# Negated maxima of the first six heads on ScalarE's DMA queue instead of SyncE's

## The chip, the cores and the metric

The kernel runs on one core of one Trainium2 chip. The core has five engines with an instruction queue each: TensorE (PE in the profile, with its weight loads as PEld), VectorE (DVE), ScalarE (ACT), GpSimd (POOL) and SyncE (SP), which computes nothing and only issues DMAs. Transfers that SP or ACT issue run on the same 16 DMA engines, on a queue for each issuer (q1 and q10 of the profile). The metric is the device time of one execution in microseconds (us); smaller is better.

## The reference

Block-sparse attention over 4 x 8 heads of 768 positions and 64 features, then a feed-forward layer on the 3072 tokens:

```python
scores = scale * np.matmul(q, k.transpose(0, 1, 3, 2))
...
scores = np.where(mask, scores, -1000000000.0)
scores = scores - np.max(scores, axis=-1, keepdims=True)
attn = np.exp(scores)
attn = attn / (np.sum(attn, axis=-1, keepdims=True) + 1e-09)
return np.matmul(attn, v).astype(np.float32)
...
h = x @ w_in
g = h - np.tanh(h)
return (g @ w_out).astype(np.float32)
```

The maximum of each query's scores is subtracted ahead of the exponential. The change concerns the way on which those maxima reach TensorE.

## The kernel before

There are 32 heads, two to a pair `pr`. A pair's transposed queries and keys lie in one of three buffers, `slot0` to `slot2` (`pr % 3`), each with four parts `sA`, `sB`, `sC`, `sD`: the masked high words, and products of high and low words for more precision. `sA` has a row of ones (row 88), and row 88 of `sB` holds the negated maximum of each query. A score is the sum of two matmuls: one over `sC` and `sD` (128 rows), one over rows 0 to 88 of `sA` and `sB` (89 rows). The second adds the negated maximum within the contraction, so it cannot start before that row has been written.

The maxima of a head come from a first pass over its scores, ahead of the second one:

- `smax` (PE): matmuls over rows 0 to 87 (88 rows in the profile) into one of six PSUM banks.
- `most` (DVE): a maximum over each bank, tile `mc`; `most_join` (DVE) joins six columns, tile `mj`.
- `most_turn` (PE): transposes `mj`, so that 6 x 128 values lie along rows.
- `most_send` (DVE, then SP): negates and shifts them into tile `nm`, and issues a DMA of 6 x 128 floats (3 KB) from `nm` into row 88 of `sB`.

The second pass of a head is three steps `n` of three tiles each: `scores` (PE), `exps` (ACT, tile `pe`, 512 columns each), `high` (ACT, tile `ph`, a 16-bit copy, two to a step), `low` (POOL, tile `pl`), `accum` (PE, over `ph`, `pl` and the values `vhl`), and at a head's end `norm` (DVE). The first passes run ahead of the second by `LEAD`, less so at the start (`RAMP`).

Nearly all other transfers stand on SP's queue: loads of queries and keys (`rawx`) and values (`rawv`), copies of `rawx` and of its low words `lo` into the slots (`dist`), and the attention results on their way to memory (`xscr<-xq`, from `spill`). Before the change ACT issues four loads at the start and one store at the end.

The order is set by hand. `at(time, f, args)` files a call under a due time, in steps of which two make one `n`; the list is sorted by time, and a helper (the line L91 that nearly all rows of the profile have) keeps each engine's instructions in the order in which they are written. An engine works its queue in order: an instruction that waits holds all behind it. A DMA has one more wait, because each takes the next of eight completion semaphores (DMAHW0 to DMAHW7) in the order of the program, over both queues, and must find that the last user of that semaphore has landed.

The pattern repeats for all heads to the end of the attention (the last nm is issued at 346.2 us); after that come the feed-forward units, which the change leaves as they are.

Of the kernel before, what the change touches and what calls it, by code (L numbers as in the profile page):

```python
# [64 lines left out]
TAIL, LASTN = 90, 93  # L65
SPIN = (-40, 14), (-1.95, 6), (-0.2, 2), (3.1, 3), (3.5, 1)
RAMP, NRAMP = 4, 24
LATE = {2: (10, 10, 6), 3: (8, 9, 3), 4: (5, 8, 2), 5: (2, 4, 1), 6: (1, 2, 0.5)}

THR2 = 0.16  # L70
# [34 lines left out]
@with_exitstack  # L105
def attention_ffn(ctx, tc, kq, v, samp, w_in, w_out, blocks, out):
    nc = tc.nc
    cst = ctx.enter_context(tc.tile_pool(name="cst", bufs=1))
    dpool = ctx.enter_context(tc.tile_pool(name="dpool", bufs=1, space=DRAM))
    xscr = [dpool.tile([P, T, DM], F32, name=f"xscr{b}") for b in range(B)]  # L110

    ident = cst.tile([P, P], F32, name="ident")
    make_identity(nc, ident)
    bias = [cst.tile([P, 1], F32, name=f"bias{i}") for i in range(2)]
    for x, val in zip(bias, (QB, THR2)):
        nc.vector.memset(x, val)

    slots = [cst.tile([P, 4, 2, S], F32R, name=f"slot{i}") for i in range(NSLOT)]
    wt = {(m, ft): dpool.tile([P, 512], F32, name=f"w{m}{ft}") for ft in range(NPRE) for m in "io"}
    part = [dpool.tile([P, DM], F32, name=f"part{j}") for j in range(CT)]  # L120
    f2 = ctx.enter_context(tc.tile_pool(name="f2", bufs=2))
    px = ctx.enter_context(tc.tile_pool(name="px", bufs=2))
    ffn = FFN(tc, w_in, w_out, xscr, ident, bias, slots, wt, out, f2, part, px)
    psum = ctx.enter_context(tc.tile_pool(name="psum", bufs=1, space=PSUM))
    banks = [psum.tile([P, 512], F32, name=f"ps{i}") for i in range(8)]
    ffn.banks, ffn.hb, ffn.cv, ffn.xt = banks[:4], banks[4:6], banks[6], banks[7]
    with ExitStack() as actx:
        turn = iter(range(10**6))
        ps = lambda n=6: banks[next(turn) % n], banks[6:]
        ffn.nc = InOrder(tc)  # L130
        attention(actx, tc, kq, v, samp, w_in, w_out, blocks, xscr, ident, ps, slots, wt, px, f2, ffn)
        ffn.nc = InOrder(tc, InOrder.ENGINES[:4])
    with ExitStack() as fctx:
        ffn.rest(fctx)


def attention(ctx, tc, kq, v, samp, w_in, w_out, blocks, xscr, ident, ps, slots, wt, px, f2, ffn):
    nc = InOrder(tc)
# [164 lines left out]
    mcs, sms = {}, {}  # L303
# [30 lines left out]
    def most_send(h):  # L334
        pr, j = divmod(h, 2)
        nm = p2.tile([T, P], F32R, tag="nm", name=f"nm{h}")
        nc.vector.tensor_scalar(out=nm, in0=mcs.pop(h), scalar1=-1.0, scalar2=8.0 * PBITS * math.log(2.0), op0=ALU.mult, op1=ALU.add)
        nc.sync.dma_start(
            out=sB[pr % NSLOT].bitcast(F32)[88:89, j, :].rearrange("o (t c) -> o t c", t=T), in_=nm.bitcast(F32)
        )  # L340

# [72 lines left out]
    def at(time, f, *args):  # L414
        ev.append((time, len(ev), f, args))
# [19 lines left out]
    for pr in range(NPAIR):  # L435
        t0 = 12 * pr
        late = LATE.get(pr, (0, 0, 0))
        at(t0 - 34.2 + late[0] if pr > 1 else -26.6 if pr else -49, load_x, pr)
# [27 lines left out]
    def smt(n):  # L466
        return 2 * n - LEAD + RAMP * max(0, 1 - n / NRAMP)

    for h in range(2 * NPAIR):
        t0 = smt(3 * h + 2)  # L470
        late = 0 if h < 4 else 0.8
        at(t0 + (2.65 if h > 4 else 1.6), most_join, h)
        at(t0 + 2.5 + late, most_turn, h)
        at(t0 + 2.75 + late, most_send, h)
        for step in range(3):
            at(6 * h + 10.3 + 0.5 * step, norm, h, step)
    for n in range(6 * NPAIR):
# [378 lines left out]
```

## Time and profile before

| what | value |
|---|---|
| three timed runs | 892.28, 892.74, 894.45 us, median 892.74 |
| the profiled execution, its own time | 895.38 us |
| its span, first to last instruction | 893.6 us |
| mean granted clock of TensorE | 0.998 |
| transfers on SP's queue (q1) | 95.31 MB, 86764 packets |
| transfers on ACT's queue (q10) | 1.05 MB, 464 packets |
| share of the chain that ended last | PE 80%, DVE 10%, DMA 5% |

In a row of a timeline stand the start, the length, the engine (SPq and ACTq are DMA issues), the operation, the tiles out and in, and the count of merged instructions; in brackets the engine's idle time before it and what ended it. Tile names leave out buffer numbers. Times count from the start of the span.

### The profile page before, as it was taken

The numbers are of one execution on the slowest core, as the hardware profiler recorded it, in microseconds if no ns is written. First come the engines' busy times: TensorE is split into PE (matmuls) and PEld (weight loads), VectorE is DVE, ScalarE is ACT, GpSimd is POOL, SyncE is SP. The second block draws the span as 40 slices with busy tenths as digits, with TensorE's granted clock in tenths as the row PEclk, the third lists the DMA queues.
The fourth block names the chain that finished last, engine by engine and source line by source line (L and its number), as shares of the span: only waits on it lengthen the run. The fifth ranks groups of instructions, "written<-read, shape, count | busy, mean of one in ns | idle before, by whom it ended". The sixth has DMA issues, their size and how long they took to land.

```text
span 893.6 us, 18523 instructions
## 1 busy us (share of the span) xinstructions
PE 875.4 (98%) x7078; PEld 734.8 (82%) x7078; DVE 717.8 (80%) x1262; ACT 648.6 (73%) x1080; POOL 505.8 (57%) x266
## 2 busy tenths in 40 slices
PE   7899999999999999999999999999999999999997
PEld 6778878888888888878888888888888888888885
DVE  8888899999999988998997687676668666866664
ACT  5799989999999999777776655565556555555553
POOL 7788989999999995677775222222222222222222
PEclk9999999999999999999999999999999999999999
DMA  6787788887888865347420202120102010001001
GB/s 182 191 212 182 182 218 206 204 210 193 211 214 222 199 173 175 117 142 225 140 76 34 63 7 66 30 34 15 47 5 34 10 47 1 1 1 48 0 1 47
DMA packets 87316, 97.53 MB, mean 109 GB/s; under 512 B 41764, under 2 KB 62436, under 8 KB 87228
## 3 DMA queue, kind: packets, MB, share of 16 engines
q1 hardware_dynamic: 86764, 95.31, 40.9%
q10 hardware_dynamic: 464, 1.05, 0.5%
q8 instruction: 55, 0.90, 0.4%
q14 instruction: 33, 0.27, 0.1%
HBM read 44.64 MB, written 15.20 MB: 67 GB/s over the span
## 4 chain that ended last, share of the span: by engine, by line
PE 80%; DVE 10%; DMA 5%; issue 2%; ACT 2%; POOL 1%; SPq 1%; ACTq 0%; DVEq 0%; POOLq 0%
PE ps L91 80%; DVE mc L91 4%; DVE ps L91 2%; DMA rawx<-kq 1%; DMA slot<-nm 1%; DVE lo L91 1%; DMA stage<-w_out 1%; DMA slot<-rawx 1%; ACT pe L91 1%; DMA rawv<-v 1%; SPq L91 1%; ACT ph L91 1%; DVE xq L91 1%; DVE pl L91 1%; DVE cvti L91 0%
## 5 line engine op out<-in xcount | busy, mean ns | idle before, releaser
L91 POOL TENSOR_TENSOR pl<-pe,ph 128x1536 f16<-128x1536 f32 x90 | 287.2, 3206 | 33.6 <-ACT ph L91 22.0
L91 POOL TENSOR_TENSOR gl<-t,gh 128x512 fp32r<-128x512 f32 x96 | 125.0, 1302 | 309.0 <-ACT gh L91 293.0
L91 PE MATMUL ps<-slot 128*128 128x512 f32 (+5 forms) x1224 | 257.7, 355 | 9.0 <-DMA slot<-nm 2.2
L91 PEld LDWEIGHTS ps<-slot 128*128 128x128 f32 (+2 forms) x1224 | 186.8, 191 | 38.0 <-DVE mc L91 4.1
L91 DVE TENSOR_REDUCE mc<-ps 128x1 f32<-128x512 f32 (+1 forms) x288 | 192.4, 680 | 21.4 <-PE ps L91 20.0
L91 ACT ACTIVATE u<-ps 128x512 f32<-128x512 f32 x96 | 57.4, 598 | 197.7 <-PE ps L91 197.7
L91 ACT ACTIVATE pe<-ps 128x512 f32<-128x512 f32 x288 | 164.0, 586 | 17.6 <-PE ps L91 14.4
L91 PE MATMUL ps<-slot,wx 128*128 128x512 f32 x720 | 173.0, 389 | 0.0
L91 ACT ACTIVATE ph<-pe 128x768 f16<-128x768 f32 x187 | 157.6, 843 | 5.4
L91 PEld LDWEIGHTS ps<-slot,wx 128*128 128x128 f32 x720 | 135.2, 188 | 28.0
L91 PE MATMUL ps<-wx,gh 128*128 128x512 f32 x480 | 147.9, 389 | 0.0
L91 PEld LDWEIGHTS <-ph 128*128 128x128 f16 x2304 | 112.6, 97 | 16.1 <-issue 13.1
L91 DVE TENSOR_TENSOR t<-t,ps 128x512 f32<-128x512 f32 x74 | 50.7, 685 | 88.1 <-ACT t L91 88.1
L91 PE MATMUL ps<-vhl,ph 128*128 128x65 f16 (+1 forms) x2304 | 120.6, 195 | 0.0
L91 PE MATMUL ps<-vhl,pl 128*128 128x65 f16 x1152 | 116.3, 193 | 0.6 <-DVE pl L91 0.3
L91 PEld LDWEIGHTS <-pl 128*128 128x128 f16 x1152 | 107.2, 100 | 1.0 <-POOL pl L91 0.6
L91 PEld LDWEIGHTS ps<-wx,gh 128*128 128x128 f32 x480 | 90.1, 188 | 18.5
L91 PE MATMUL ps<-wx,gl 128*128 128x512 f32 x240 | 93.5, 389 | 0.0
L91 DVE COPY_PREDICATED t<-mk,ps 128x512 f32<-128x512 int32 x96 | 71.3, 743 | 6.7 <-ACT mk L91 0.4
L91 DVE TENSOR_TENSOR ps<-ps,u 128x512 f32<-128x512 f32 x96 | 66.6, 694 | 11.5 <-ACT hs L91 11.4
L91 DVE SCALAR_TENSOR_TENSOR ps<-qq,ps 128x512 f32<-128x512 f32 x96 | 66.6, 694 | 8.0 <-DVE ps L91 0.5
L91 PE MATMUL ps<-slot,slot 128*128 128x512 f32 x288 | 69.6, 391 | 0.6 <-DVE t L91 0.6
(103 smaller groups left out, 1186.6 us busy)
## 6 DMA issues: line engine op xcount, KB each, us to landing
slot<-rawx SPq DMA_DIRECT2D x31, 384.0 KB, 7.1
slot<-lo SPq DMA_DIRECT2D x62, 192.0 KB, 3.1
slot<-rawx SPq DMA_DIRECT2D x61, 192.0 KB, 4.1
rawx<-kq SPq DMA_DIRECT2D x15, 768.0 KB, 6.1
stage<-w_in SPq DMA_DIRECT2D x13, 512.0 KB, 3.8
stage<-w_out SPq DMA_DIRECT2D x13, 512.0 KB, 4.0
rawv<-v SPq DMA_DIRECT2D x16, 384.0 KB, 5.3
xscr<-xq SPq DMA_DIRECT2D x16, 384.0 KB, 3.6
```

What stands on the lines that cost most here:

```text
L91: r = f(*args, **kw)
```

## The change

The transfer leaves `most_send` and becomes a call of its own, `most_dma`. For heads 0 to 5 it is issued by ACT and filed 0.3 later than the negation; for the other 26 heads it stays on SP at the same due time.

```diff
+EARLYH = 6
...
-        nc.sync.dma_start(
+        mcs[h] = nm
+
+    def most_dma(h):
+        pr, j = divmod(h, 2)
+        nm = mcs.pop(h)
+        (nc.scalar if h < EARLYH else nc.sync).dma_start(
             out=sB[pr % NSLOT].bitcast(F32)[88:89, j, :].rearrange("o (t c) -> o t c", t=T), in_=nm.bitcast(F32)
         )
...
         at(t0 + 2.75 + late, most_send, h)
+        at(t0 + 2.75 + late + (0.3 if h < EARLYH else 0), most_dma, h)
```

The order of the instructions on TensorE, VectorE and GpSimd stays the same; those of ACT and SP differ at the six transfers. Three places show it. Each row is an instruction with its tiles, and in brackets the semaphores that it waits for: an engine's name for that engine's, DMAHW with a number for a transfer's. The line number of the helper is L91 before and L92 now.

SP's queue at the first head, before: the loads of pair 1's keys and queries and pair 0's values, the two copies of pair 0's low words, the transfer of `nm0`, and the first copies for pair 1.

```order
L91 DMA rawx1_173<-kq 128x1536 [waits DMAHW1_49]
L91 DMA rawv0_175<-v 128x768 [waits DMAHW2_49]
L91 DMA slot0_73<-lo0_160 64x768 [waits DMAHW3_49,Pool_49]
L91 DMA slot0_73<-lo0_160 64x768 [waits DMAHW4_49]
L91 DMA slot0_73<-nm0_232 1x6x128 [waits DVE_49]
L91 DMA slot1_74<-rawx1_173 64x2x768 [waits DMAHW1_49]
L91 DMA slot1_74<-rawx1_173 64x2x768 [waits DMAHW7_49]
```

The same place of SP's queue now.

```order
L92 DMA rawx1_173<-kq 128x1536 [waits DMAHW1_49]
L92 DMA rawv0_175<-v 128x768 [waits DMAHW2_49]
L92 DMA slot0_73<-lo0_160 64x768 [waits DMAHW3_49,Pool_49]
L92 DMA slot0_73<-lo0_160 64x768 [waits DMAHW4_49]
L92 DMA slot1_74<-rawx1_173 64x2x768 [waits DMAHW1_49]
L92 DMA slot1_74<-rawx1_173 64x2x768
```

The transfer of `nm0` is gone from SP, and the copies for pair 1 follow the low words directly. The numbers also show how the semaphores are dealt: 1, 2, 3, 4 to four transfers in turn, so the first copy of the low words has number 3.

ACT's queue at the same head, between the placing of pair 0's low words and the first exponentials, now (before, the row of `nm0` isn't there, and the others stand in the same order):

```order
L92 ACTIVATE slot0_73<-slot0_73 64x768 [waits DMAHW7_49]
L92 ACTIVATE slot0_73<-lo0_160 64x768 [waits Pool_49] x2
L92 DMA slot0_73<-nm0_232 1x6x128 [waits DMAHW3_49,DVE_49]
L92 ACTIVATE pe0_255<-ps2_97 128x512 [waits PE_49]
L92 ACTIVATE pe0_255<-ps4_99 128x512 [waits PE_49]
```

On ACT the transfer waits for VectorE, as before, and also for number 3, which belongs to the first copy of the low words.

ACT's queue at head 1, before: the end of step 1 and the start of step 2, whose exponentials are `pe2`.

```order
L91 ACTIVATE ph1_309<-pe1_294 128x768 [waits Activation_49]
L91 ACTIVATE pe1_294<-ps3_98 128x512 [waits PE_49]
L91 ACTIVATE ph1_309<-pe1_294 128x768 [waits Activation_49]
L91 ACTIVATE pe2_336<-ps2_97 128x512 [waits PE_49]
L91 ACTIVATE pe2_336<-ps4_99 128x512 [waits DVE_49,PE_49]
```

The same place now.

```order
L92 ACTIVATE ph1_309<-pe1_294 128x768 [waits Activation_49]
L92 ACTIVATE pe1_294<-ps3_98 128x512 [waits PE_49]
L92 ACTIVATE ph1_309<-pe1_294 128x768 [waits Activation_49]
L92 DMA slot0_73<-nm1_328 1x6x128 [waits DMAHW0_49,DVE_49]
L92 ACTIVATE pe2_336<-ps2_97 128x512 [waits PE_49]
L92 ACTIVATE pe2_336<-ps4_99 128x512 [waits PE_49]
```

The transfer of `nm1` stands between the last copy of step 1 and the exponentials of step 2, and both wait for it to be issued. The transfers of heads 2, 3 and 5 also stand directly behind a `ph` copy on ACT, that of head 4 behind the third `pe` of step 10.

## The prediction

> **What bounds the kernel now.** I read the busy times of the page first, then busy time by stretch, then the chain of waits, then single engines' timelines.
>
> ```profile
> PE 875.4 (98%) x7078; PEld 734.8 (82%) x7078; DVE 717.8 (80%) x1262; ACT 648.6 (73%) x1080; POOL 505.8 (57%) x266
> 14.00:27.00 13.00, 9.93 (x55) 7.51 (x53) 12.50 (x26) 8.74 (x14) 10.43 (x10) 1.00 0.81 219
> 27.00:33.00 6.00, 3.69 (x49) 2.92 (x50) 5.49 (x10) 2.96 (x5) 5.61 (x2) 1.00 1.05 247
> 90.00:110.00 20.00, 19.69 (x275) 16.88 (x274) 17.55 (x36) 19.25 (x30) 19.09 (x7) 1.00 0.70 170
> 130.00:180.00 50.00, 49.54 (x690) 42.59 (x687) 47.51 (x100) 47.98 (x75) 46.27 (x15) 1.00 0.83 211
> 400.00:600.00 200.00, 199.78 (x882) 164.87 (x881) 156.20 (x244) 129.86 (x235) 91.14 (x72) 1.00 0.29 77
> ```
>
> The stretches give PE, PEld, DVE, ACT and POOL busy, then the granted clock, the DMA engines' share and GB/s. TensorE works 875.4 of 893.6 us, and from 130 us on it hardly pauses (49.54 of 50, 199.78 of 200). So an early delay or gain is a shift that is carried to the end; the early stages decide. From 14 to 27 us VectorE is the bound (12.50 of 13) and TensorE idles 3.07 us; from 27 to 33 us TensorE idles 2.31 us.
>
> Next, who waits for the moved transfers (tile nm), and two pieces of the chain of waits (start, length):
>
> ```profile
> L91 SPq DMA_DIRECT2D slot<-nm x32: 730/747/797, 15.5 to 346.2; - x32
>   PE ps L91: 2.2, 2
> 27.08 5.04 DMA slot<-nm
> 61.53 6.00 DMA slot<-nm
> 32.16 1.60 PE L91 MATMUL ps<-slot 89*128 89x512 f32 x7 [1.61 <-DMA slot<-nm]
> 67.57 1.10 PE L91 MATMUL ps<-slot 89*128 89x512 f32 x5 [0.57 <-DMA slot<-nm]
> ```
>
> TensorE waits twice for nm, 2.2 us in all: 1.61 us for head 1 (issued 27.08, landed 5.04 us later) and 0.57 us for head 4 (61.53, 6.00 us). That is the pool from which the change can draw directly. Heads 2, 3 and 5 make nobody wait.
>
> The first stall costs twice. These stretches of 3.41 us lie on the clock's own steps:
>
> ```profile
> 19.65:23.06 3.41, 2.64 (x14) 1.86 (x13) 3.17 (x8) 3.35 (x6) 1.39 (x1) 1.00 0.90 232
> 26.48:29.89 3.41, 2.50 (x44) 1.99 (x43) 3.38 (x7) 3.18 (x5) 3.11 (x1) 1.00 1.04 267
> 29.89:33.30 3.41, 1.80 (x11) 1.29 (x10) 2.94 (x5) 0.59 (x3) 3.10 (x1) 1.00 1.04 235
> 33.30:36.71 3.41, 3.41 (x42) 2.89 (x41) 1.38 (x3) 2.71 (x5) 0.56 (x1) 0.50 0.78 171
> ```
>
> The stretch with the stall has TensorE busy for 1.80 of 3.41 us, and the next one runs at clock 0.50 throughout, with TensorE as the bound: 3.41 x 0.5 = 1.7 us lost. A stretch with 2.50 busy was not followed by that.
>
> **Part 1, heads 1 and 4: faster landing.** On SP, nm stands behind bulk loads in one queue. On ACT's queue nothing stands before it. What such a transfer takes there is not in the trace; the bounds are a lone one and a queued one:
>
> ```profile
> 16.00:18.00 2.00, 1.16 (x6) 0.71 (x5) 1.86 (x4) 0.03 (x1) 2.00 (x4) 1.00 0.27 60
> 15.46 0.80 SPq L91 DMA_DIRECT2D slot<-nm  x1
> 16.88 1.05 PE L91 MATMUL ps<-slot 128*128 128x512 f32 x2 [0.76 <-DMA slot<-lo]
> 17.43 0.19 PEld L91 LDWEIGHTS ps<-slot 89*128 89x128 f32 x1 [0.40 <-DMA slot<-nm]
> 27.70 0.95 PE L91 MATMUL ps<-slot 128*128 128x512 f32 x3 [0.91 <-DVE mc L91]
> ```
>
> Head 0's took 17.43 - 15.46 = 1.97 us while the DMA engines were mostly idle (0.27 from 16 to 18 us); the other end is 6.00. I take 2.5, nearer the lone one, since the queue is empty though the DMA engines are not. Head 1 needs it within 32.16 - 1.61 - 27.08 = 3.47 us, so its 1.61 us go; head 4 within 6.00 - 0.57 = 5.4, so its 0.57 go. The half-clock stretch goes with the first: another 1.7 us of this execution.
>
> By the Trainium skill, DMA: Bandwidth & Descriptors, section Issuing engines are not separate DMA queues, starting DMAs from several engines saves only the sequencer's time, usually small beside the DMA. By that rule the 5.04 and 6.00 us would stay, and with them both stalls. The section on queues, rings and completion order of the same page says that SP and ACT own a ring each on every DMA engine and that the engines go round between rings, which would let nm pass the bulk loads. No run here shows either yet.
>
> **Part 2, head 0: later issue.** Each transfer takes the next of eight completion semaphores and waits until that one's last user has landed. With nm now later in the program's order, head 0's gets the semaphore of the first lo transfer (DMAHW3 in the rows ahead), where before it waited for VectorE alone. TensorE's wait for lo ends at 16.88, so ACT issues at about 16.8 rather than 15.46: 1.34 us later. With the 2.5 us from above instead of 1.97, head 0's scores start at about 19.3 instead of 17.43: **1.9 us late** (bounds: 1.34, and 16.8 + 6.00 - 17.43 = 5.4). Queued behind that matmul on TensorE are the maxima matmuls of head 1, and VectorE waits for those:
>
> ```profile
> 17.03 2.59 DVE L91 TENSOR_REDUCE mc<-ps 128x1 f32<-128x512 f32 x4
> 26.78 0.27 DVE L91 TENSOR_SCALAR nm<-ps 6x128 fp32r<-6x128 f32 x1
> 13.01 1.11 SPq L91 DMA_DIRECT2D slot<-lo  x2
> 16.30 4.87 SPq L91 DMA_DIRECT2D slot<-rawx  x4
> ```
>
> VectorE is full there (12.50 of 13), so nearly all of the 1.9 us reaches head 1's nm at 26.78 and TensorE's matmul at 27.70, which waits for VectorE. It is a loss in full against the 1.61 won. SP, freed of nm, can send the rawx copies right behind the lo issues, which end at 14.12, instead of at 16.30; nobody waits for them, but they load the DMA engines while nm travels, which is why I don't take 1.97.
>
> The longer gap can also cost clock. TensorE would idle 0.76 + 1.9 = 2.7 us around 16 to 19.3, more than the 1.61 before 33 us. A half-clock stretch then holds 1.71 of the 2.64 us of work that stands in 19.65 to 23.06: 0.9 us late (bounds 0, if none follows, and 1.7). I take 0.9.
>
> By the Trainium skill, TensorE: Matmul & The Clock Gate, Part 1, the clock falls to half after an idle window of about 3.4 us. The trace differs: 1.80 of 3.41 us busy was enough. By the page's rule this term would be nil and the forecast 892.7.
>
> **Part 3, ACT's time.** Six issues at 0.75 us move to ACT's sequencer:
>
> ```profile
> SPq L91 <- DVE mc L91: 23.5, 6, 8.6
> 0.75 2.48 ACTq L91 DMA_DIRECT2D rawx<-kq  x4
> 25.59 0.85 ACT L91 ACTIVATE ph<-pe 128x768 f16<-128x768 f32 x1
> 26.34 1.09 ACT L91 ACTIVATE pe<-ps 128x512 f32<-128x512 f32 x2
> 32.75 1.08 ACT L91 ACTIVATE pe<-ps 128x512 f32<-128x512 f32 x2 [2.81 <-PE ps L91]
> 50.34 0.84 ACT L91 ACTIVATE ph<-pe 128x768 f16<-128x768 f32 x1
> 51.09 0.58 ACT L91 ACTIVATE pe<-ps 128x512 f32<-128x512 f32 x1
> ```
>
> An issue on ACT took 2.48 / 4 = 0.62 us in the one place that the trace shows. Head 0's falls into ACT's idle time before its first exponential. Head 1's blocks ACT from 26.44 until nm is made (26.78 + 0.27 = 27.05) and 0.75 more: the exponentials at 26.34 start near 27.8, 1.5 us late, and 2.81 us of idle time behind them take that up. Heads 2 to 5 come where ACT is full. Each activation starts before the last one ends (26.34 against 25.59 + 0.85 = 26.44), so ACT's sequencer is an instruction ahead, and heads 2, 3 and 5 stand right behind a ph copy of 0.84 us that covers 0.75. I take 0.2 us for the four, bounds 0 and 4 x 0.75 = 3.0. SP loses waits of up to 8.6 us for maxima (23.5 in all), and its loads go earlier; as no engine waits for those loads in these stretches, I count nothing for it. If that cover were gone, a load would show as a wait in the stretches up to 80 us.
>
> **Sum.** Against the profiled execution (895.38 us: span 893.6 and 1.8 around it): -1.61 - 0.57 - 1.7 + 1.9 + 0.9 + 0.2 = -0.9, so 894.5. That execution lies 2.64 us above the median of the runs shown (892.74). The three runs are 892.28, 892.74 and 894.45; I read the gap of about 2 us as the half-clock stretch, present in the third and in the profiled run and absent at the median. Then 1.7 of the 2.64 is not there to be won, and the other 0.9 is profiling's own offset: 894.5 - 0.9 = **893.6 us**. In the same terms, the median gains 2.18 and loses 3.0.
>
> **The rivals.**
> - *Cheap head 0.* nm lands near 1.97 us, and no half clock follows its gap: -2.18 + 1.34 + 0.2 = -0.6, so 892.1; if VectorE's slack hides even the 1.34, 890.6. For it: ACT's queue is empty. Against: VectorE's 12.50 of 13, and 0.81 DMA share in that stretch. Stages bound by ACT up to 110 us (19.25 of 20) may swallow some of it.
> - *Loaded landing* (ends slower). On ACT's queue nm still takes 5.04 us, because the DMA engines are loaded and not because of the place in a queue. Head 0 is then 16.8 + 5.04 - 17.43 = 4.4 us late, head 1's stall stays but for 0.04, and head 4's goes: 4.4 - 0.04 - 0.57 + 0.9 + 0.2 = +4.9, so 897.6. Each 1 us of landing costs 1 us, and twice that from 3.47 us on; the sum passes +2.7 at a landing of 3.9 us. For it: SP's loads now start before nm. Against: 1.97, and the queue of its own.
> - *Bare ACT time.* The sequencer isn't ahead, and four issues cost 3.0 where ACT is full: 893.6 + 2.8 = 896.4. For it: 19.25 of 20. Against: the overlapped starts.
> - *The change does nothing for the landing.* Each head's landing stays what it was on SP (1.97, 5.04, 6.00): head 0 pays 1.34, both stalls remain, and 0.2 is added: 894.3.
>
> **How the numbers follow.** Chances: forecast 0.56 (own range 891.5 to 895.3), cheap head 0 0.20, loaded landing 0.11, bare ACT time 0.08, no effect on the landing 0.05. A measurement of this kernel can tell about 0.3% (2.7 us) from no change. Faster than 890.06 is only the far end of cheap head 0: 0.06. Slower than 895.42 are most of loaded landing (0.09) and of bare ACT time (0.06) and a tail of the forecast (0.01): 0.16. The rest, 0.78, is within. The range runs from 890.5 (all of cheap head 0 but its tail) to 896.5 (bare ACT time), and leaves out loaded landing.
>
> **What would show it.** Right: head 0's first 89-row matmul moves from 17.43 to 18.7 or later, waiting for nm; the waits of 1.61 and 0.57 are gone; nm's issues stand on ACT's queue with no new idle time of ACT behind them from 40 to 75 us; a clock of 0.50, if any, stands near 19 to 24 us and not at 33. Wrong: landings on ACT's queue of 4 us and more, a wait for nm still at 32 us, PE waiting for ACT's pe or ph by more than 1 us between 42 and 76 us, or head 0 no later than before.

## The result, and the profile after

The changed kernel takes 902.18 us (median of 4 runs, 900.24 to 902.77), the kernel before 892.51 (4 runs, 892.10 to 894.45): ratio 1.0101, 95% interval 1.0082 to 1.0119. It is slower by 1%, where 893.6 and no measurable change were forecast. The profiled execution takes 901.92 us, with a span of 900.1.

The waits for nm come first. The views are the answer on the tile nm (issues with their count and minimum, median and maximum in ns; waits in us with their count), the chain of waits (start, length) and TensorE's timeline.

```profile
L92 ACTq DMA_DIRECT2D slot<-nm x6: 677/692/1282, 16.9 to 79.2; - x6
  PE ps L92: 6.2, 2
```

```profile
16.93 4.87 DMA slot<-nm
42.91 6.07 DMA slot<-nm
```

```profile
21.84 2.50 PE L92 MATMUL ps<-slot 89*128 89x512 f32 x8 [4.38 <-DMA slot<-nm]
49.03 3.47 PE L92 MATMUL ps<-slot 89*128 89x512 f32 x11 [1.82 <-DMA slot<-nm]
```

There are two waits again, but others: head 0 (4.38 us) and head 2 (1.82 us) in place of head 1 (1.61) and head 4 (0.57), 6.2 us instead of 2.2. The transfers of heads 0 and 2 needed 4.87 and 6.07 us on a queue on which nothing stood before them.

The first three stretches are those of the prediction's table, the fourth is the one in which it read a DMA share of 0.27; below them stand three of the clock's own steps. All are of the kernel after:

```profile
14.00:27.00 13.00, 7.22 (x31) 5.60 (x30) 7.25 (x16) 3.35 (x5) 5.25 (x7) 0.74 0.94 259
27.00:33.00 6.00, 4.30 (x26) 3.24 (x24) 5.89 (x12) 4.94 (x8) 5.56 (x3) 1.00 0.16 35
130.00:180.00 50.00, 48.74 (x681) 41.82 (x681) 46.70 (x100) 47.30 (x74) 43.84 (x15) 1.00 0.80 202
16.00:18.00 2.00, 0.59 (x3) 0.19 (x1) 1.92 (x4) 0.00 (x0) 2.00 (x4) 1.00 0.96 221
18.69:22.10 3.41, 0.26 (x1) 0.26 (x2) 0.00 (x0) 0.00 (x0) 0.56 (x1) 0.50 1.05 237
22.10:25.52 3.42, 3.42 (x13) 3.03 (x14) 1.83 (x3) 2.04 (x3) 0.00 (x0) 0.50 1.00 347
49.41:52.83 3.42, 3.42 (x21) 2.71 (x20) 1.68 (x3) 2.54 (x5) 3.42 (x2) 0.50 0.91 187
```

From 14 to 27 us VectorE works 7.25 us instead of 12.50, and TensorE 7.22 instead of 9.93. Three steps run at clock 0.50. The DMA engines are at 0.94 there instead of 0.81, at 0.96 instead of 0.27 from 16 to 18, and at 0.16 from 27 to 33, where before they stood at 1.05: the loads have moved forward, into the time in which head 0's nm travels.

SP's queue shows why, around head 2. Before:

```profile
30.35 0.73 SPq L91 DMA_DIRECT2D slot<-rawx  x1
39.16 0.74 SPq L91 DMA_DIRECT2D slot<-nm  x1
39.95 0.43 SPq L91 DMA_DIRECT2D rawx<-kq  x1
40.42 2.71 SPq L91 DMA_DIRECT2D slot<-rawx  x4
```

```profile
39.00:41.00 2.00, 2.00 (x43) 1.85 (x42) 1.56 (x6) 1.88 (x3) 0.27 (x1) 1.00 0.02 5
```

After:

```profile
35.63 0.54 SPq L92 DMA_DIRECT2D rawx<-kq  x1
36.21 6.30 SPq L92 DMA_DIRECT2D slot<-rawx  x5
42.85 0.84 ACT L92 ACTIVATE ph<-pe 128x768 f16<-128x768 f32 x1
42.91 0.68 ACTq L92 DMA_DIRECT2D slot<-nm  x1
```

```profile
42.90:49.00 6.10, 4.30 (x64) 3.53 (x60) 4.67 (x12) 5.54 (x8) 3.23 (x2) 1.00 0.99 217
```

Before, SP reached nm after the issue of a copy at 30.35 and stood there until VectorE had made nm at 39.13. For those 8 us nothing behind it was issued, the DMA engines emptied (0.02 from 39 to 41), and nm went ahead of the loads. After, SP does not wait for nm: pair 3's load and the copies are issued from 35.63 on, ahead of nm at 42.91, and the DMA engines are at 0.99 while it travels. So the wait on SP's queue, which looked like lost time, had kept the way free for nm.

### The profile page after: what moved, and what is told of

Read it like the earlier page. It is cut to its first block, busy times and chain, and to the rows that moved or that the text cites. A ratio compares the mean times of both kernels' runs of the same rounds, so it can differ in the third digit from the quotient of the medians.

```text
span 900.1 us, 18528 instructions
## 1 busy us (share of the span) xinstructions
PE 876.3 (97%) x7078; PEld 735.1 (82%) x7078; DVE 717.7 (80%) x1262; ACT 649.0 (72%) x1080; POOL 505.3 (56%) x266
## 4 chain that ended last, share of the span: by engine, by line
PE 81%; DVE 9%; DMA 4%; issue 2%; ACT 2%; POOL 1%; SPq 0%; ACTq 0%; DVEq 0%; POOLq 0%
PE ps L92 81%; DVE mc L92 3%; DVE ps L92 2%; DMA slot<-nm 1%; DVE pl L92 1%; DMA rawo<-w_out 1%; ACT pe L92 1%; DMA rawv<-v 1%; ACT ph L92 1%; DVE lo L92 1%; DVE xq L92 0%; DMA rawx<-kq 0%; DMA wo<-cvto 0%; DVE ph L92 0%; DVE cvti L92 0%
## 5 line engine op out<-in xcount | busy, mean ns | idle before, releaser
L92 POOL TENSOR_TENSOR pl<-pe,ph 128x1536 f16<-128x1536 f32 x90 | 287.0, 3203 | 40.3 <-ACT ph L92 24.8
L92 POOL TENSOR_TENSOR gl<-t,gh 128x512 fp32r<-128x512 f32 x96 | 124.6, 1298 | 309.2 <-ACT gh L92 293.2
L92 PE MATMUL ps<-slot 128*128 128x512 f32 (+5 forms) x1224 | 259.6, 357 | 14.2 <-DMA slot<-nm 6.2
L92 PEld LDWEIGHTS ps<-slot 128*128 128x128 f32 (+2 forms) x1224 | 188.4, 192 | 43.2 <-DMA slot<-nm 7.0
L92 DVE TENSOR_REDUCE mc<-ps 128x1 f32<-128x512 f32 (+1 forms) x288 | 192.1, 678 | 27.6 <-PE ps L92 26.2
L92 ACT ACTIVATE u<-ps 128x512 f32<-128x512 f32 x96 | 57.6, 600 | 197.6 <-PE ps L92 197.6
L92 ACT ACTIVATE pe<-ps 128x512 f32<-128x512 f32 x288 | 164.1, 587 | 23.7 <-PE ps L92 19.0
L92 PE MATMUL ps<-slot,wx 128*128 128x512 f32 x720 | 172.9, 389 | 0.0
L92 ACT ACTIVATE ph<-pe 128x768 f16<-128x768 f32 x187 | 157.6, 843 | 5.6
L92 PEld LDWEIGHTS ps<-slot,wx 128*128 128x128 f32 x720 | 135.2, 188 | 28.0
L92 PE MATMUL ps<-wx,gh 128*128 128x512 f32 x480 | 147.8, 389 | 0.0
L92 PEld LDWEIGHTS <-ph 128*128 128x128 f16 x2304 | 111.9, 97 | 16.2 <-issue 13.2
L92 DVE TENSOR_TENSOR t<-t,ps 128x512 f32<-128x512 f32 x74 | 50.6, 684 | 88.3 <-ACT t L92 88.3
L92 PE MATMUL ps<-vhl,ph 128*128 128x65 f16 (+1 forms) x2304 | 119.9, 194 | 0.0
L92 PE MATMUL ps<-vhl,pl 128*128 128x65 f16 x1152 | 115.6, 192 | 1.1 <-POOL pl L92 0.8
L92 PEld LDWEIGHTS <-pl 128*128 128x128 f16 x1152 | 106.8, 99 | 1.4 <-POOL pl L92 1.0
L92 PEld LDWEIGHTS ps<-wx,gh 128*128 128x128 f32 x480 | 90.1, 188 | 18.6
L92 PE MATMUL ps<-wx,gl 128*128 128x512 f32 x240 | 93.4, 389 | 0.0
L92 DVE COPY_PREDICATED t<-mk,ps 128x512 f32<-128x512 int32 x96 | 71.1, 741 | 6.7 <-ACT mk L92 0.4
L92 DVE TENSOR_TENSOR ps<-ps,u 128x512 f32<-128x512 f32 x96 | 66.6, 693 | 11.5 <-ACT hs L92 11.4
L92 DVE SCALAR_TENSOR_TENSOR ps<-qq,ps 128x512 f32<-128x512 f32 x96 | 66.6, 694 | 8.1 <-DVE ps L92 0.5
L92 PE MATMUL ps<-slot,slot 128*128 128x512 f32 x288 | 69.5, 390 | 0.6 <-DVE t L92 0.6
```

Of the source, the lines that this page charges most:

```text
L92: r = f(*args, **kw)
```

## The experiments

The theory after the two traces is that the place of nm among the loads counts, not the queue or the engine that issues it. Its rivals: ScalarE's queue is slow by itself; ScalarE's own time for the issues; the wait for a completion semaphore; the half clock. Times are medians, and the difference in us is against the runs of the kernel before on the same chip.

| run | us | minus before | 95% interval of the ratio |
|---|---|---|---|
| head0_back | 899.00 | +6.27 | 1.0059 to 1.0083 |
| head0_alone | 897.78 | +5.05 | 1.0046 to 1.0072 |
| held_loads | 897.96 | +5.23 | 1.0042 to 1.0078 |
| heads_1_4 | 897.76 | +5.03 | 1.0043 to 1.0069 |
| head1_alone | 893.03 | +0.41 | 1.0001 to 1.0018 |
| head2_alone | 896.43 | +3.81 | 1.0026 to 1.0051 |
| held_until_landed | 896.19 | +3.57 | 1.0024 to 1.0050 |
| nm0_behind_loads | 898.82 | +6.20 | 1.0058 to 1.0085 |
| heads_0_2_held | 896.27 | +3.68 | 1.0028 to 1.0053 |
| head0_filled | 900.59 | +8.00 | 1.0077 to 1.0104 |
| loads_behind_nm1 | 897.74 | +5.15 | 1.0043 to 1.0068 |
| copies_behind_nm1 | 891.90 | -0.47 | 0.9984 to 1.0010 |
| head0_filled_less | 896.54 | +4.17 | 1.0039 to 1.0081 |

### Which heads cost: head0_alone, head2_alone, head1_alone, head0_back

The edit is to the changed kernel, here for head 0 alone; `2,`, `1,` and `1, 2, 3, 4, 5` are the other three.

```diff
-EARLYH = 6
+EARLYH = 0,
...
-        (nc.scalar if h < EARLYH else nc.sync).dma_start(
+        (nc.scalar if h in EARLYH else nc.sync).dma_start(
...
-        at(t0 + 2.75 + late + (0.3 if h < EARLYH else 0), most_dma, h)
+        at(t0 + 2.75 + late + (0.3 if h in EARLYH else 0), most_dma, h)
```

> Only head 0's transfer on ScalarE's queue, heads 1 to 5 on SyncE's as before. Theory L: landing again over 4 us, TensorE waits about 4.4 us for it, half clock at 19 to 25 us; the small stalls of heads 1 and 4 may stay. 896 to 899, i.e. 4 to 6 us over the kernel before. Rival S (the wait for the semaphore of the first copy of the low words, 1.4 us, is what head 0 pays, and the long landing of the one profile was chance): 893.5 to 894.5, landing about 2 us. Rival A: no loss, within 0.5 us of before.

> Only head 2's transfer on ScalarE's queue; before it made nobody wait (made 39.13, issued 39.16, last packet 1.46 us later). Theory P: ScalarE comes to it 0.7 to 0.9 us late, behind a ph copy, and with SyncE's loads no longer held behind it the last packet comes 4 to 7 us after the issue; TensorE waits 1.5 to 4 us for it and a half-clock step of 3.4 us follows; 895.5 to 899. If the loss in the changed kernel was handed on from head 0 and head 2 is late only because of it: within 1 us of the kernel before.

> Only head 1's transfer on ScalarE's queue, where with heads 1 and 4 moved it was issued as soon as it was made (27.14, issued 27.17) and removed the wait at 32 us. Theory P (a transfer on ScalarE's queue loses its place: it is issued when ScalarE's queue comes to it, and its packets share the DMA engines with loads that on SyncE's queue would stand behind it; a head wins only where neither happens): head 1 alone wins its 1.61 us or a part, and the later heads, which are on SyncE's queue again, keep landing in under 2 us but for head 4; 890.5 to 892.7. Rival (any transfer on ScalarE's queue costs, by ScalarE's time or by a mixture of queues): 894 or more.

> Head 0's transfer back on SyncE's queue, heads 1 to 5 stay on ScalarE's. Theory L (a maximum that leaves on ScalarE's queue meets the bulk loads that SyncE, no longer held by it, sends at the same moment; heads 0 and 2 pay): head 0's 4.38 us wait of TensorE and the half-clock steps at 19 to 25 us go; head 1 lands in under 3.5 us, so the 1.61 us of before stay away; head 2's wait near 49 us (1.82 us) and its half-clock step stay. 902.2 less about 5.5: 895 to 898. Rival Q (ScalarE's queue is slow by itself, 3 to 6 us whatever the load): the same here, so this run doesn't part them. Rival A (ScalarE's own time for the issues): heads 1 to 5 still cost it, 900 or more.

Head 0 alone costs 5.05 us, within the theory's range; its nm takes 5.33 us and TensorE waits 4.85 (chain, then TensorE):

```profile
17.11 5.33 DMA slot<-nm
```

```profile
22.48 1.86 PE L92 MATMUL ps<-slot 89*128 89x512 f32 x6 [4.85 <-DMA slot<-nm]
```

Head 2 alone costs 3.81 us, though in the kernel before it made nobody wait:

```profile
32.62 4.50 SPq L92 DMA_DIRECT2D slot<-rawx  x4
38.22 0.84 ACT L92 ACTIVATE ph<-pe 128x768 f16<-128x768 f32 x1
38.28 1.29 ACTq L92 DMA_DIRECT2D slot<-nm  x1
45.53 2.93 PE L92 MATMUL ps<-slot 89*128 89x512 f32 x9 [2.97 <-DMA slot<-nm]
```

```profile
38.28 7.21 DMA slot<-nm
```

```profile
44.91:48.32 3.41, 2.79 (x10) 2.50 (x11) 0.87 (x2) 1.24 (x3) 3.41 (x2) 0.50 0.01 3
48.32:51.74 3.42, 3.42 (x41) 2.80 (x40) 1.37 (x3) 2.13 (x3) 2.15 (x2) 0.50 0.02 5
```

The four copies leave at 32.62 and nm at 38.28 behind them; it lands after 7.21 us, TensorE waits 2.97, and two steps at half clock follow. So head 2's loss is its own and not handed on from head 0. This execution is the slowest of its five (898.88) and has one more step at half clock, from 17.61 to 21.02, ahead of anything that the edit touches: the trace shows the kind of loss, the median its size.

Head 1 alone wins nothing (+0.41). In this execution its nm takes as long on ScalarE's queue as on SP's in the profile of before (5.04), and TensorE waits as it did there (1.61):

```profile
27.15 5.10 DMA slot<-nm
```

```profile
32.30 0.98 PE L92 MATMUL ps<-slot 89*128 89x512 f32 x5 [1.67 <-DMA slot<-nm]
```

This was the larger of the two savings that the change could make, and a queue of its own does not make it in the median; my expectation of a win was wrong here. With head 0 back on SP, 899.0 came out above the 895 to 898 expected: head 2 then makes TensorE wait 3.94 us instead of 1.82. The costs do not add up. Heads 0, 2 and 1 alone cost 5.05 + 3.81 + 0.41 = 9.27 of 9.67, but heads 1 to 5 together cost 6.27, and heads 1 and 4 together, below, 5.03, of which head 1 alone is 0.41. So head 4 costs about 4.6 us there, though in the profile of after it makes nobody wait.

### The place or the engine: nm0_behind_loads

All transfers on SP, head 0's filed later, so that three copies of rawx leave ahead of it:

```diff
-        (nc.scalar if h < EARLYH else nc.sync).dma_start(
+        nc.sync.dma_start(
...
-        at(t0 + 2.75 + late + (0.3 if h < EARLYH else 0), most_dma, h)
+        at(t0 + 2.75 + late + (0 if h else 1.08), most_dma, h)
```

> All transfers on SyncE's queue as before, only head 0's filed behind three of the four copies of rawx for pair 1, which then leave first; ScalarE issues nothing new. Theory P: the place among the loads is what counts, not the engine that issues: issued near 16.6 us, last packet 3 to 5 us later, TensorE waits 3 to 4.5 us, half clock near 19 to 25 us, 896 to 899 as with head 0 alone on ScalarE's queue (897.78). Rival Q: on SyncE's queue it lands in 2 to 2.5 us, 893.5 to 895.

```profile
14.76 2.71 SPq L92 DMA_DIRECT2D slot<-rawx  x3
17.56 1.48 SPq L92 DMA_DIRECT2D slot<-nm  x1
22.84 1.44 PE L92 MATMUL ps<-slot 89*128 89x512 f32 x4 [5.05 <-DMA slot<-nm]
```

```profile
17.56 5.23 DMA slot<-nm
```

ScalarE issues nothing new here, and the loss is the same and a little more: 5.23 us of landing against 5.33 on ScalarE's queue, a wait of 5.05 against 4.85, and +6.20 us. Nor does this nm wait for a completion semaphore: by the trace's records the last user of the one dealt to it had landed at 11.95. This is the run that decides for head 0: it is the place among the loads.

### Holding SP's loads back: held_loads, held_until_landed, heads_0_2_held

A copy of each maximum to scratch memory, on SP at the old place, makes SP wait for the maximum again (first diff). In the second the copy reads the written row, so that SP waits until nm has landed; the third does this for heads 0 and 2, the only ones on ScalarE's queue there.

```diff
         mcs[h] = nm
+        if h < EARLYH:
+            nc.sync.dma_start(out=held[h], in_=nm.bitcast(F32))
+
+    held = [dpool.tile([T, P], F32, name=f"held{i}") for i in range(EARLYH)]
```

```diff
+    held = [dpool.tile([1, S], F32, name=f"held{i}") for i in range(EARLYH)]
...
+        if h < EARLYH:
+            nc.sync.dma_start(out=held[h], in_=sB[pr % NSLOT].bitcast(F32)[88:89, j, :])
...
-        at(t0 + 2.75 + late + (0.3 if h < EARLYH else 0), most_dma, h)
+        at(t0 + 2.75 + late + 0, most_dma, h)
```

> As the changed kernel, and SyncE also sends a copy of each of the six maxima to scratch memory at the place where the real transfer stood before, so that its loads stay held until the maximum exists; head 0's transfer then also has a semaphore whose last user landed long ago. Theory L: head 0 is issued near 15.5 us and lands within 2.5 us, head 2 within 3 us; both new waits of TensorE (4.38 and 1.82 us) and the half-clock steps behind them go; time 889.5 to 893, at or below the kernel before. Rival Q: landings on ScalarE's queue stay 3 to 6 us though SyncE holds its loads, waits of 2 us and more, 897 or more. Rival A: 899 or more, since ScalarE still issues six.

> As the changed kernel, but SyncE holds its further loads until each of the six maxima has landed (it copies the written row to scratch memory and has to wait for it). Theory P: with no load started behind it the last packet of each comes within 2 to 3 us of the issue, also for heads 2 and 4 (5.26 and 2.35 in the changed kernel, 4.14 and 6.40 where the loads were held only until the maximum was made); what is left are the late issues on ScalarE's queue (0.4 to 2.8 us for heads 2 and 4) and loads that start 2 us later than before; TensorE waits for nm under 1.5 us in all, 891 to 895. Rival Q (ScalarE's queue is slow by itself): last packets 3 to 7 us after the issue as before, 896 or more.

> Heads 0 and 2, the two that cost 5.1 and 3.8 us alone, on ScalarE's queue, with SyncE's further loads held until each of the two has landed; the other heads on SyncE's queue. Theory P: last packets 1.4 to 1.6 us after the issue (as in the run where all six were held: 1.52 and 1.40), no wait of TensorE for either, 892 to 894.5, with some of it for loads that start 2 us later. Rival Q: the queue itself or ScalarE's time costs it, 896 or more, towards the sum of 8.9 us.

The chain of held_loads:

```profile
15.46 1.93 DMA slot<-nm
37.67 5.56 DMA slot<-nm
63.38 7.08 DMA slot<-nm
```

Head 0 now goes at 15.46 and lands after 1.93 us on ScalarE's queue, as on SP (1.97). So that queue is not slow by itself, and head 0's 89-row matmuls start at 17.43, as before. But a hold up to the making of nm is not enough, as SP's rows around head 2 show:

```profile
36.80 0.29 SPq L92 DMA_DIRECT2D held<-nm  x1
37.14 0.33 SPq L92 DMA_DIRECT2D rawx<-kq  x1
37.51 2.81 SPq L92 DMA_DIRECT2D slot<-rawx  x4
```

ScalarE, busy with a ph copy, issues nm only at 37.67, 0.9 us after it is made; by then SP has sent pair 3's load and the first copy, and nm takes 5.56 us. Head 4 comes 1.3 us after its making, behind the landing of its semaphore's last user at 63.31, and takes 7.08. TensorE waits 1.49 and 3.33 us for the two, and 897.96 stands where 893 or less was expected. That time lies where a slow queue would have put it; it is head 0's 1.93 us that speaks against one.

With the hold up to the landing, TensorE's matmuls wait neither for head 0 nor for head 2 in either run, and head 2's last packet comes 1.40 and 1.43 us after its issue on ScalarE's queue. In held_until_landed, where ScalarE still issues all six, head 1's is the only nm that TensorE's matmuls wait for, 2.46 us. In heads_0_2_held the waits are head 1's, 3.03, and head 4's, 0.84, both on SP's queue. The rows at head 1:

```profile
17.36 0.25 SPq L92 DMA_DIRECT2D held<-slot  x1
17.71 4.50 SPq L92 DMA_DIRECT2D slot<-rawx  x4
27.02 0.80 SPq L92 DMA_DIRECT2D slot<-nm  x1
33.54 2.93 PE L92 MATMUL ps<-slot 89*128 89x512 f32 x8 [3.03 <-DMA slot<-nm]
```

```profile
27.02 6.47 DMA slot<-nm
```

The copies start at 17.71 instead of 16.30, and 27.02 finds more of the loads still under way: 6.47 us of landing instead of 5.04, a wait of 3.03 instead of 1.61. The mechanism was right for the held heads and the expected times too low (896.2 and 896.3 instead of 891 to 895 and 892 to 894.5): the loads have to pass somewhere, and pushing them behind one nm puts them ahead of the next. Head 1's longer wait does not account for all of the 3.6 us; what else costs is not shown, and ScalarE's time for the issues may be a part of it.

### An issue that comes late on ScalarE: heads_1_4

The edit is `EARLYH = 1, 4`, the two heads that waited before.

> Only heads 1 and 4, the two that made TensorE wait before, on ScalarE's queue. Theory L: each 1 us of landing under the old one is won where it stalled; landings of about 3 us (2.78 and 3.17 in the changed kernel) remove the 1.61 and 0.57 us and the half-clock step behind the first: 889 to 892. Against that, SyncE's loads behind these two are freed as well; if they delay a neighbour, 893 to 895. Rival A: two issues at 0.7 us, 892 to 894.

```profile
54.14 0.58 SPq L92 DMA_DIRECT2D xscr<-xq  x1
58.80 0.27 DVE L92 TENSOR_SCALAR nm<-ps 6x128 fp32r<-6x128 f32 x1
60.55 0.58 ACT L92 ACTIVATE pe<-ps 128x512 f32<-128x512 f32 x1
61.88 0.74 ACTq L92 DMA_DIRECT2D slot<-nm  x1
67.31 3.01 PE L92 MATMUL ps<-slot 89*128 89x512 f32 x9 [2.42 <-DMA slot<-nm]
```

In this execution head 1 landed after 3.73 us, and the wait at 32 us is all but gone (0.28). Up to there the program is that of head1_alone, which took 5.10: two executions differ by that much. Head 4 gave the gain back: nm is made at 59.07 (58.80 + 0.27) and issued only at 61.88. Until 61.13 ScalarE works through what stands ahead of it, the third pe of its step last. After that it still waits for a landing, by the trace's semaphore records: its completion semaphore was last used by the store xscr<-xq, which SP issued at 54.14 and which landed at 61.80. This is the wait that the prediction counted for head 0, whose issue at 16.93 in the profile of after follows such a landing at 16.85. The 30 transfers of nm that SP issues in this trace all follow the making by 0.03 us. Once issued, head 4's needs 5.39 us, and TensorE waits 2.42 instead of 0.57. The expectation (889 to 892) was wrong by 6 us; it had taken no account of where ScalarE would be, nor of the semaphore.

### The half clock: head0_filled, head0_filled_less

Idle matmuls ahead of head 0's first scores keep TensorE busy in the wait; 40 more in the first, 20 in the second (the diff is the second's). Both have head 0 alone on ScalarE's queue.

```diff
-SPIN = (-40, 14), (-1.95, 6), (-0.2, 2), (3.1, 3), (3.5, 1)
+SPIN = (-40, 14), (-1.95, 6), (-0.2, 22), (3.1, 3), (3.5, 1)
```

> Head 0 alone on ScalarE's queue (897.78), with 40 more idle matmuls of 0.11 us on TensorE ahead of the first scores, which fill about 4.5 us of its wait. Theory C (part of the cost of a wait is the half clock that follows it): no half-clock step between 18 and 28 us, and the work behind the wait goes at full clock; 1.0 to 2.5 us won, 895.3 to 896.8. If VectorE, full in that stretch, hides the half clock: 897.5 to 898.5 with the clock at 1.00.

> Head 0 alone on ScalarE's queue (897.78), with 20 more idle matmuls ahead of the first scores instead of 40. A matmul there took 0.22 us and not 0.11, so the 40 ended at 25.05 us, 2.65 us after the maxima's usual arrival; 20 end near 20.6 and leave a wait of about 1.5 us. Theory C: no half-clock step between 18 and 28 us; with 40 the scores began 2.65 us later than with none and step 9 only 1.50 us later, so full clock is worth about 1.1 us: 896.2 to 897.2. If the idle matmuls change nothing but the clock's record: 897.4 to 898.4.

The same 10 us in head0_alone, head0_filled and head0_filled_less:

```profile
18.00:28.00 10.00, 5.51 (x20) 4.87 (x21) 3.84 (x9) 3.71 (x6) 1.35 (x3) 0.66 0.88 237
```

```profile
18.00:28.00 10.00, 10.00 (x82) 9.40 (x80) 3.32 (x7) 2.29 (x4) 1.25 (x2) 1.00 0.91 243
```

```profile
18.00:28.00 10.00, 8.28 (x55) 6.81 (x53) 5.39 (x12) 5.58 (x9) 3.38 (x3) 1.00 0.84 230
```

Forty overshot: TensorE was filled until 25 us, and the kernel lost time (900.59). With twenty the clock stays at 1.00 and the median is 896.54 instead of 897.78; but the two intervals in the table overlap, and one of the six runs took 902.96, so the times do not show the gain beyond doubt. In the two profiled executions the scores began 0.82 us earlier with the fill (21.66 against 22.48), the exponentials of step 9 began 1.83 us earlier (57.92 against 59.75), and the span is 1.2 us shorter (894.8 against 896.0). What goes beyond the 0.82 us is 1.0 at step 9 and 0.4 at the end: from this one pair I estimate the half clock at 0.4 to 1 us of head 0's 5. The rest is the wait.

### Order on SP's queue alone: loads_behind_nm1, copies_behind_nm1

The kernel before, with loads of pair 1 filed behind head 1's nm: in the first the values and two copies, in the second the two copies only.

```diff
-    NEXT = -1.3, -0.6, -0.4, -0.8, 1, 2, 3, 4, 6, 7
+    NEXT = -1.3, -0.6, -0.4, -0.8, 4.02, 4.04, 3, 4, 6, 7
...
-        at(t0 - 15.5 if pr > 1 else 1 if pr else -26.5, load_v, pr)
+        at(t0 - 15.5 if pr > 1 else 4.03 if pr else -26.5, load_v, pr)
```

> The kernel before, with nothing on ScalarE's queue; three loads of pair 1 (values, and the copies of rawx for its second head) that stood ahead of head 1's transfer on SyncE's queue stand behind it. Theory P (place among the loads): head 1 lands 1.5 to 3.5 us after its issue instead of 5.04, its wait of 1.61 us goes, and the time is 890 to 892.5 unless the three loads, late by 4 us, are waited for in turn. Rival: the landing of head 1 is set by other loads (the rest of pair 2's load, issued at 21.2), and nothing changes: 892.3 to 893.

> The kernel before, nothing on ScalarE's queue; of the loads ahead of head 1's transfer on SyncE's queue only the two copies of rawx for pair 1's second head stand behind it, the values stay ahead, so that VectorE does not wait 3.38 us for them as it did with the values moved too. Theory P: less stands ahead of head 1, which lands 2 to 4 us after its issue instead of 5.04; its wait of 1.61 us goes wholly or in part; 890.5 to 892.3. Rival (the rest ahead, pair 2's load of 0.79 MB and the values, sets the landing, or the moved copies are waited for later): 892.3 to 894.

With all three moved, head 1's wait is gone, but VectorE waits for the values, which a reduction needs at 31.9 us, and the kernel is 5.15 us slower where 890 to 892.5 was expected:

```profile
35.26 0.95 DVE L91 TENSOR_REDUCE am<-rawv 128x1 f32<-128x768 f32 x1 [3.38 <-DMA rawv<-v]
```

With only the copies moved, the answer on the tile nm of copies_behind_nm1 has one wait of TensorE, and its timeline shows that it is head 0's:

```profile
  PE ps L91: 0.4, 1
17.39 1.45 PE L91 MATMUL ps<-slot 89*128 89x512 f32 x8 [0.39 <-DMA slot<-nm]
```

For head 1 TensorE does not wait: its last packet comes 1.48 us after the issue at 27.03, against 3.89 us in the profile of before. So order on SP's queue does remove what the change was meant to remove. The time is 891.90 against 892.37, and the interval includes no change. If moving the copies costs nothing elsewhere, that wait costs at most about 1.4 us in a usual run (the lower end, 0.9984), less than the 3.3 us that the profiled execution of before suggested with its half-clock step. No version here beats the kernel before beyond doubt.

## Why the prediction was wrong, point by point

- **The frame held in the main.** An early delay is carried to the end: head 6's nm is made 5.74 us later (88.52 instead of 82.78), the last one at 352.4 instead of 345.9 us, and the spans differ by the same 6.5 us. Most of what comes after head 6 falls between 130 and 180 us, where TensorE is busy 0.80 us less (48.74 against 49.54); why is not shown. The medians differ by 9.67, mainly because the profiled execution of before lay 2.9 us above its median.
- **The step from that execution to the median is not borne out.** It explained 1.7 us by a half-clock stretch and called 0.9 profiling's own offset. But runs of the kernel before with a mean clock of 0.995 took 892.50 and 892.64 us, and runs at 1.000 up to 894.32; and the profiled execution of after (901.92) lies below its median. In the rival of a cheap head 0 the far end is 892.1 - 1.34 = 890.8, not 890.6.
- **Part 1 failed** in its landing of 2.5 us on ScalarE's queue. I took the empty queue for a short way. Lone, nm takes 1.93 us there, but at heads 0 and 2 it took 4.87 and 6.07, and head 1 alone took 5.10 against 5.04 on SP. Head 1's landing varies on either queue: 3.73 and 5.10 on ScalarE's, and on SP's 5.04 against less than 3.7 in head2_alone, where it is issued later, at 27.89, and the matmul starts at 31.57. That the waits of heads 1 and 4 did vanish in the profile of after is no support: by then head 1's nm was 5.4 us later (32.52 instead of 27.08), behind a stretch with the DMA engines at 0.16. By the Trainium skill, DMA: Bandwidth & Descriptors, section Issuing engines are not separate DMA queues, transfers of all issuers interleave on the same engines and another issuer saves only its sequencer's time; the runs agree with it (5.33 on ScalarE's queue and 5.23 on SP's for a loaded head 0, 1.93 and 1.97 for a nearly lone one). I had set what the Trainium skill says in the section on queues, rings and completion order of that page against it, and hoped that alternating between rings would let 3 KB pass. No run shows it passing.
- **Part 2 had the mechanism and the wrong size.** Head 0 was forecast 1.9 us late and is 21.84 - 17.43 = 4.41 late. The later issue is 16.93 - 15.46 = 1.47 of it (forecast 1.34); the landing adds 4.87 - 1.97 = 2.9 (forecast 0.53). The half-clock term, 0.9, lies within the 0.4 to 1 us of the filled run, though two steps at half clock stand there and not one.
- **Part 3's step "its loads go earlier ... I count nothing for it" failed** most. I asked only who waits for the loads, not what they meet. They meet nm: head 2, at which nobody waited, got a wait of 1.82 us and a step at half clock, and costs 3.8 us alone. Of ScalarE's time the forecast was right where nm stands behind a ph copy (42.91 within 42.85 to 43.69). The wait for the completion semaphore, which Part 2 has for head 0, also held head 4 back in heads_1_4, 2.81 us together with ScalarE's work ahead of it; for that there was no term.
- **The rival that came true for head 0** is the loaded landing, at 0.11. It gave 897.6, with a landing of 5.04 us where head 0 had 4.87. It lacked 4.6 us to 902.18 and did not have head 2, which costs 3.8 alone; that head 2 is most of the 4.6 is likely but not shown, since the single costs do not add up.
- **Open:** what the late issue of head 0 alone, by the semaphore's wait, would cost without the loads (no run parts the two; by the sum above it is a third of the 4.41 us); how the costs of heads 1, 2 and 4 combine to 6.27 us for heads 1 to 5; and why head 1's landing differs between executions.

## What to carry to other kernels

By these runs, an instruction that blocks a DMA queue can be the flow control that keeps the DMA engines free for what it waits for: before moving it, ask which loads it holds and where they will go. Here a queue of its own did not give a small transfer a way of its own; its place in time among the bulk loads did, and that could be set by order on one queue. A landing read from a lone transfer is no estimate for a loaded stretch: take it from the DMA share at the time of the issue.

## What the runs showed of the hardware

Issuing nm from ScalarE took 0.68 to 0.74 us, but the first nm that ScalarE issued in each trace took 1.27 to 1.45, whichever head it was (0, 1 or 2).

The half-clock step does not follow each wait of the same length: head 1's 1.61 us in the profile of before was followed by one, its 1.67 us in head1_alone was not. The Trainium skill, TensorE: Matmul & The Clock Gate, Part 1, has windows of about 3.4 us that run freely; the steps here are 3.41 us long and agree with that. But the place of the gap within a step does not part these two executions: counted back in steps of that length from head1_alone's change of clock at 889.00 us, the step from 28.84 to 32.25 holds nearly all of its wait and has TensorE busy for 1.79 us, against 1.80 before. The busy time alone does not decide either. Half clock followed a step with 2.12 us busy (head2_alone, 14.19 to 17.61) and did not follow one with 1.99 (head0_alone, 13.61 to 17.03). What decides stays open.
